# Gated linear attention and a low-rank mixer on one core: gates kept as logarithms on 64 partitions, decay matrices by one matmul and an Exp, scores and state products on four 64x64 tiles

## The chip, the cores and the metric

The kernel runs on one core of a Trainium2 chip. Its engines are TensorE (PE, with its weight loads as PEld), VectorE (DVE), ScalarE (ACT), GpSimd (POOL) and the queues that issue transfers (SP's and ACT's). The metric is the device time of one launch in microseconds (us).

## The reference

Two stages. First a recurrent attention over 768 steps for 4 batches and 8 heads of 40 channels; then a token mixer of rank 32 and an MLP 320 -> 1280 -> 320 over the 320 channels of each token. All in float32.

```python
for t in range(S):
    m_new = np.maximum(f_gate[:, :, t] + m, i_gate[:, :, t])
    f_stab = np.exp(f_gate[:, :, t] + m - m_new)
    i_stab = np.exp(i_gate[:, :, t] - m_new)
    m = m_new
    C = f_stab[:, :, None, None] * C + i_stab[:, :, None, None] * np.einsum('bhd,bhe->bhde', vt, kt)
    n = f_stab[:, :, None] * n + i_stab[:, :, None] * kt
    h_tilde = np.einsum('bhde,bhe->bhd', C, qt)
    denom = np.maximum(np.abs(np.einsum('bhd,bhd->bh', n, qt)[:, :, None]), 1.0)
    y[:, :, t] = o * h_tilde / denom          # o = sigmoid(o_gate)
...
u = x + (x.T @ U @ V).T                       # x: y with the heads side by side
out = u + np.maximum(u @ w_ch1, 0.0) @ w_ch2
```

## The kernel before

The recurrence is done in blocks of 64 steps: 768 steps are two halves (`hf`) of 384, a half is six blocks (`NQ`). Within a block the output is a masked product of scores (q times k), weighted with the decay between the two steps, times v (`pv`); what comes from earlier blocks goes through the state C (`inter`). The heads lie in two groups `m` of four, one on partitions 0 to 63, one on 64 to 127, so that one instruction on 128 partitions serves two heads; `i` counts the four pairs.

The work of a batch b and half hf, in the program's names:

- the gates, once for all batches, on 32 partitions for each half: scans for the running maximum, two exps, two more scans (`gate_max`, `gate_w`, `gate_g`), then products with the identity that turn the factors to token-major order (`tok`, `dect`).
- the decay matrix of a pair (128x384): a row of forget factors is spread over 64 partitions, for the first 12 pairs by a TensorE product with a one-column selector (`rowmm`, tensor `fst`), later by a broadcast transfer (`fd<-fsd`); then a scan on DVE (`decay_scan`, L753) runs along each row. The weight of the state (`gst`, `gsd`) is spread the same way and multiplied on q (`q_decay`, L748).
- `scores`: 12 products of 40 rows by 64x64 for a pair, on two of the four 64x64 tiles of TensorE; `weigh` (L772) multiplies them with the decay; `pv` and `inter` add into two PSUM banks on all four tiles; `kv` (k times v of a block, two tiles) and `state` (L694, L696) carry C from block to block.
- `norm`, `out_norm`, `gate` give x for a half (L825, L831). Then `rows` multiplies x with U (as two F32R parts), `cols` adds V's part and transposes x into `ut`, and the MLP follows as `up` (8 F32R products of 128x384 for each of 10 slices) and `down` (9 of 128x320). Weights come as float64 words and are turned into a high and a low F32R part by DVE and ACT (`cv`, L519, L521).

The order is not the code's order. `Plan` collects operations with a priority and an assumed cost, and `schedule` lists them engine by engine before the kernel is built; each engine then works its list strictly in order. Where TensorE would be idle by the planner's reckoning, it puts in products of zeros (`zeros`, fillers), which keep the engine active. PSUM has two pools, three banks for `down` and five for all else.

Of the kernel before, what the change touches and what calls it, by code (L numbers as in the profile page):

```python
# [19 lines left out]
RANK = 32  # L20
# [10 lines left out]
DMP = 3 * P  # L31


REBASE = 2.0 ** -112
SIGNED = -(2.0 ** 32)

# [8 lines left out]


FB_FROM, GB_FROM = 12, 8
LAG = 2
CV0, CV1, CV2 = 53.6, 80.0, 95.3
TICK, TICK_COLUMNS, FILL_NS, FILL_COLUMNS = 5120.0 / 3, 1900.0, 107.0, 256.0  # L50
RP, MP = 75.4, 175.5
GP = 21.3
ALT_PRI = 94.9
FILL_SLACK, FORCE, FILL_TO = 0.8, True, 2200.0

ORDER = {
    "gate": 20.0, "gate_w": 10.0, "part2": -70.0, "out_norm": -30.0, "part1": -10.0, "gate_turn": 10.0, "part3":
    -30.0, "rest1": 2.0, "w_low": 30.0, "vi": -10.0, "state": -4.0, "load_tk": -20.0, "w13_low":
    -30.0,
}  # L60
ORDER0 = {
    "rows": 25.0, "inter": 3.0, "x_low": -10.0, "weigh": 10.0,
}
BEGIN, COLD, FIRST_DMA, PE_SETUP = 600.0, 4500.0, 1700.0, 2200.0
DELTA = {"pe": 0}

WIDE_DMA = 630.0
# [7 lines left out]
    "prr": (1, [P, DM], F32R),  # L75
    "rru": (1, [P, HS], F32R),
    "kv": (2, [P, 2 * 3 * NP * (D + DV)], F32),
    "og": (2, [P, 2 * 3 * NP * D], F32),
    "v2": (1, [P, 2 * 3 * NP * DV], F32),
    "qd": (3, [Q + D, HS], F32),  # L80
    "qk": (3, [Q + D, 2, HS], F32),
    "C": (5, [Q + D, 3 * NP * DV], F32),
    "dm": (2, [P, HS], F32),
    "wt": (2, [P, HS], F32),
    "fd": (3, [P, HS], F32),
    "rd": (2, [P, 3 * NP], F32),
    "o": (3, [P, DM], F32),
# [4 lines left out]
BANKS = {"m2": 3, "ps": 5}  # L92
SHARE = {"dc": ("ps", 2), "st": ("ps", 5), "at": ("ps", 5), "m1": ("ps", 5)}
# [5 lines left out]
class Plan:  # L99


    def __init__(self, slots):
        self.slots = {tag: [[tile, 0.0, None, tag] for tile in tiles] for tag, tiles in slots.items()}
        self.ops, self.at, self.busy, self.port = [], {}, defaultdict(float), []
# [8 lines left out]
    def op(self, kind, pri, eng, cost, fn, r=(), w=(), new=(), stream="", load=1.0, port=False):  # L113
# [27 lines left out]
        self.port.append(port or not isinstance(eng, str))  # L141

    def keep_busy(self, at, start, cost, load, filler):

        busy = self.busy
        while True:
            n = int(at // TICK)
            step = FILL_NS * (2 if at < COLD else 1)
            if busy[n] >= FILL_TO:
# [3 lines left out]
            elif at + FILL_SLACK * step <= start:  # L153
                if filler(at):
                    busy[n] += FILL_COLUMNS
                at += step
            else:
                break
        while FORCE:
# [4 lines left out]
            if lack <= gain * max(0.0, left - cost) or left < FILL_NS or not filler(start):  # L164
                break
            busy[n] += FILL_COLUMNS
            start += FILL_COLUMNS / gain
        a, z = start, start + cost * (2 if start < COLD else 1)
        while a < z:
# [3 lines left out]
            a = b + 0.01  # L173
        return start

    def schedule(self, filler, ENGINE):

        ops = self.ops
        waits = [len(set(o[4]) | set(o[5])) for o in ops]
# [9 lines left out]
        while ready:  # L189
            picks = {}  # L190
            for n, est in ready.items():
# [3 lines left out]
                for key, tag in new:  # L195
# [4 lines left out]
                    s = max(s, open_at[nth]) if len(open_at) > nth and self.held[tag] + nth < most else float("inf")  # L200
# [4 lines left out]
                if isinstance(engs, str):  # L205
                    picks.setdefault(engs, []).append((max(s, free[engs]), pri, n))
# [15 lines left out]
            if eng == "pe":  # L222
                s = self.keep_busy(free["pe"], s, cost, load, filler)
# [43 lines left out]
def mlstm_mixer_kernel(  # L267
# [42 lines left out]
    ident6 = const.tile([P, HS], F32, name="ident6")  # L310
    ones = const.tile([NBH, Q], F32, name="ones")
    zeros = const.tile([P, 512], BF16, name="zeros")


    fst = const.tile([2 * NBH, HS + 1], F32, name="fst")
    gst = const.tile([2 * NBH, HS], F32, name="gst")
# [768 lines left out]
```

## Time and profile before

| | us |
|---|---|
| median of 3 runs | 389.26 (386.53, 389.26, 389.57) |
| profiled execution, span (no other time is listed for it) | 389.8 |
| TensorE busy in it | 379.4 (97%) |
| DVE busy | 219.1 (56%) |
| ACT busy | 106.9 (27%) |
| POOL busy | 61.1 (16%) |
| transfers | 40.65 MB, 104 GB/s in the mean |

A matmul's busy time is a modelled length of the pipeline, 0.31 to 0.34 us for one that is followed by the next after half of that; so the busy share of TensorE says little, and starts of neighbouring instructions are the measure. F32 products appear twice in the trace (768 records for 384 products), F32R products once.

### The profile page before, as it was taken

How to read it: one execution, taken by the hardware profiler on the slowest of the kernel's cores; microseconds unless marked ns; L12 is line 12 of the kernel's file. 1: busy time of each engine (PE TensorE's matmuls, PEld its weight loads, DVE VectorE, ACT ScalarE, POOL GpSimd, SP SyncE). 2: the span in 40 equal slices, each digit the busy share in tenths (PEclk: the TensorE clock that was granted, in tenths of full speed). 3: DMA queues.
4: the chain of work that ended last, by engine and by line, in shares of the span. 5: the costliest groups of instructions: out<-in, count | busy, mean ns of one | idle time of the engine just before them, and what ended most of it. 6: DMA issues, size and time to landing. Idle time of an engine off the chain costs nothing. (4 is left out here: it accounts for less than half of the span.)

```text
span 389.8 us, 11285 instructions
## 1 busy us (share of the span) xinstructions
PE 379.4 (97%) x4860; PEld 336.2 (86%) x4860; DVE 219.1 (56%) x471; ACT 106.9 (27%) x240; POOL 61.1 (16%) x65
## 2 busy tenths in 40 slices
PE   8999998899999899999999999999999999999996
PEld 5566666578898899999898899998999999999996
DVE  7747888745988853459886845256620433220322
ACT  4320235505453352102143113211420322220220
POOL 1303353521425200023231200000000000000000
PEclk9859999857999999999999999999999999999999
DMA  8963968836954921126978421020000010100001
GB/s 176 183 190 108 212 182 184 246 126 132 275 168 137 227 77 50 47 96 176 225 189 207 148 62 50 2 76 4 2 0 2 1 52 0 53 0 2 25 27 50
DMA packets 23002, 40.65 MB, mean 104 GB/s; under 512 B 4200, under 2 KB 15720, under 8 KB 22952
## 3 DMA queue, kind: packets, MB, share of 16 engines
q1 hardware_dynamic: 22760, 39.70, 38.3%
q8 instruction: 38, 0.62, 0.7%
q10 hardware_dynamic: 192, 0.23, 0.2%
q14 instruction: 12, 0.10, 0.1%
HBM read 35.68 MB, written 4.23 MB: 102 GB/s over the span
## 5 line engine op out<-in xcount | busy, mean ns | idle before, releaser
L290 PE MATMUL m<-w2h,h 128*128 128x320 f32 x480 | 120.4, 313 | 0.0
L290 PE MATMUL ps<-ut,w1h 128*128 128x384 f32 x400 | 118.2, 341 | 0.6 <-DVE ut L895 0.3
L934 DVE SCALAR_TENSOR_TENSOR h<-ps,h 128x384 fp32r<-128x384 f32 x80 | 44.0, 554 | 93.4 <-ACT h L932 92.6
L290 PEld LDWEIGHTS m<-w2h,h 128*128 128x128 f32 x480 | 83.5, 188 | 0.8
L290 PE MATMUL ps<-ut,w1l 128*128 128x384 f32 x240 | 80.6, 336 | 0.0
L932 ACT ACTIVATE h<-ps 128x384 fp32r<-128x384 f32 x80 | 38.9, 491 | 150.3 <-PE ps L290 98.7
L290 PEld LDWEIGHTS ps<-ut,w1h 128*128 128x128 f32 x400 | 73.6, 188 | 2.2 <-DVE h L934 0.7
L290 PE MATMUL m<-w2l,h 128*128 128x320 f32 x240 | 73.9, 308 | 0.0
L290 PEld LDWEIGHTS m<-w2l,h 128*128 128x128 f32 x240 | 45.1, 188 | 0.0
L290 PEld LDWEIGHTS ps<-ut,w1l 128*128 128x128 f32 x240 | 45.1, 188 | 0.0
L290 PEld LDWEIGHTS <-zeros 128*128 128x128 bf16 (+1 forms) x204 | 19.9, 111 | 17.6 <-issue 11.0
L290 PE MATMUL m<-zeros 128*128 128x256 bf16 x196 | 34.1, 315 | 0.0
L290 PE MATMUL ps<-qk 40*64 40x64 f32 x768 | 31.0, 227 | 0.3 <-DMA out<-o 0.3
L290 PEld LDWEIGHTS ps<-qk 40*64 40x64 f32 x768 | 27.1, 140 | 4.4 <-issue 2.2
L772 DVE TENSOR_TENSOR wt<-ps,dm 128x384 f32<-128x384 f32 x32 | 17.7, 552 | 15.1 <-PE ps L290 14.9
L753 DVE TENSOR_TENSOR_SCAN dm<-fd,ident 128x384 f32<-128x384 f32 x20 | 20.8, 1041 | 3.5 <-DMA fd<-fsd 3.4
L290 PEld LDWEIGHTS ps<-kv,wt 64*64 64x64 f32 x768 | 15.8, 143 | 6.6 <-issue 4.2
L957 DVE TENSOR_TENSOR o<-m,x 128x320 f32<-128x320 f32 x24 | 11.0, 487 | 18.3 <-PE m L290 18.2
L290 PEld LDWEIGHTS ps<-v,kv 64*40 64x40 f32 x704 | 15.7, 119 | 5.8 <-issue 5.0
L290 PE MATMUL ps<-v,kv 64*40 64x41 f32 x704 | 17.5, 204 | 2.9 <-issue 2.8
L659 POOL TENSOR_TENSOR v<-kv,tok 128x492 f32<-128x492 f32 x10 | 10.4, 1057 | 61.2 <-PE ps L290 57.2
L290 PE MATMUL ps<-kv,wt 64*64 64x41 f32 x768 | 19.7, 238 | 0.1
(91 smaller groups left out, 403.1 us busy)
## 6 DMA issues: line engine op xcount, KB each, us to landing
kv<-in_tk SPq DMA_DIRECT2D x16, 486.0 KB
qk<-in_qk SPq DMA_DIRECT2D x64, 120.0 KB
raw<-in_w SPq DMA_DIRECT2D x20, 320.0 KB
og<-in_tk SPq DMA_DIRECT2D x16, 240.0 KB
fd<-fsd SPq DMA_DIRECT2D x40, 96.0 KB
out<-o SPq DMA_DIRECT2D x24, 160.0 KB
fd<-gsd SPq DMA_DIRECT2D x24, 96.0 KB
fd<-gsd SPq DMA_DIRECT2D x24, 80.0 KB
```

The source lines that it names most:

```text
L290: nc.tensor.matmul(o, a, b, start=start, stop=stop, **kw)
L659: p.op("v2", at(n - 1), ("pool", "dve"), (pool(VO) * 0.79, dve(VO)), lambda e, e2=e2: e.tensor_mul(v2flat()[:, e2], vflat()[:, e2], tokv(1 ...
L753: lambda kfb=kfb, kdm=kdm: nc.vector.tensor_tensor_scan(T[kdm], T[kfb][:, 0:HS], ident6, 0.0, ALU.mult, ALU.add),
L772: p.op("weigh", at(u), "dve", dve(HS), lambda ks=ks, kw=kw, kdm=kdm: nc.vector.tensor_mul(T[kw], T[ks][:, 0:HS], T[kdm]), r=[ks, kdm], w=[ ...
L932: p.op("relu_high", pri + m - 1000, "act", 371, lambda: nc.scalar.activation(T[kh][:, 0, :], T[kp][:, 0:HS], AF.Relu), r=[kp], w=[(kh, 0)] ...
L934: p.op("relu_low", pri + m - 1000, "dve", dve(HS), lambda: nc.vector.scalar_tensor_tensor(T[kh][:, 1, :], T[kp][:, 0:HS], 0.0, f32(T[kh][: ...
L957: p.op("residual", pri - 1000, "dve", dve(DM), lambda: nc.vector.tensor_add(T[ko], T[ka][:, 0:DM], T[X][:, tt, 0:DM]), r=[ka] + [(X, hf, m ...
```

## The change

- Gates: both halves lie together on 64 partitions, and stay logarithms. `G` is the running sum of the log forget factors within a block, `E` the log input gate less G. Each is split into a high and a low F32R part, and stored to DRAM (`ggd`, `eed`); `gsd` holds exp(G).
- Decay matrix of a pair: one F32R product of 80 rows (`e`: a triangular mask with a large negative number, selectors, and the loaded rows of G and E) gives the logarithm of the decay with the input gate in it, 128x384 in PSUM, and ACT's Exp writes it to `dm`. The scan, the spread rows and the product of v with the input gate (`vi`) go. The state's weight is spread by a product and an Exp in batch 0 (`g_rows`), by transfers after that.
- `scores` does two pairs at once, 24 products on four tiles and into two banks; `kv` does all six blocks at once in the same manner, ACT copies the result (`kv_keep`), and `state` works on the copy, on DVE or POOL. The order of heads on the partitions alternates (`r ^ ip`).
- POOL builds the constant rows of `e` at the start (`put`). Sigmoid becomes Tanh and a POOL step. `norm` is on DVE alone. Batch 0's `rows` is one F32 product per chunk (`rows32`).
- One PSUM pool of eight banks; the planner knows a cost for going between whole-array and tiled products (`SWITCH`), and has a new table of priorities for all operations.

```diff
-BANKS = {"m2": 3, "ps": 5}
-SHARE = {"dc": ("ps", 2), "st": ("ps", 5), "at": ("ps", 5), "m1": ("ps", 5)}
+BANKS = {"ps": 8}
+SHARE = {"m2": ("ps", 3), "m1": ("ps", 3), "st": ("ps", 2), "at": ("ps", 4), "a0": ("ps", 8), "o": ("cv", 5)}
...
+            away = SWITCH * ((self.last != "F") + (mode != "F"))
...
+        p.op("gate_sum", -89, "dve", scan(HS), lambda: V.tensor_tensor_scan(G(), begin(), f(), 0.0, ALU.mult, ALU.add),
+             r=kf + [(X0, "one")], w=[(X0, "G")], port=True)
+        p.op("gate_e", -89, "dve", dve(HS), lambda: V.scalar_tensor_tensor(E(), i(), 64 * LEAST, G(), ALU.max, ALU.subtract),
+             r=ki + [(X0, "G")], w=[(X1, "E")], port=True)
...
+        p.op("store_g", -88, "sp", dma(NG * S * 4), lambda: nc.sync.dma_start(
+            out=ggd.rearrange("r l t -> r (l t)"), in_=part(X2, 0, S)), r=[(X2, "gh"), (X2, "gl")], w=[("ggd",)])
...
+            nc.gpsimd.affine_select(
+                t[0:Q, 0:4 * HS].rearrange("p (x s) -> p x s", s=Q), one.unsqueeze(2).to_broadcast([Q, 4 * NQ, Q]),
+                [[0, 4 * NQ], [-1, Q]], ALU.is_gt, 0.0, base=0, channel_multiplier=1)
...
-                p.op(
-                    "decay_scan", at(u), "dve", scan(HS),
-                    lambda kfb=kfb, kdm=kdm: nc.vector.tensor_tensor_scan(
-                        T[kdm], T[kfb][:, 0:HS], ident6, 0.0, ALU.mult, ALU.add),
...
+                        def load_er(m=m):
+                            nc.sync.dma_start(out=f32(T[ke][64 + 2 * m:66 + 2 * m, 0:4 * HS]).rearrange("p (h s) -> p h s", s=HS),
+                                              in_=ggd[r0 + 4 * m:r0 + 4 * m + 4].rearrange("h l t -> l h t"))
...
+                    p.op("decay", at(u), "pe", 173, lambda kd=kd, i=i: mm(T[kd][:, 0:HS], el(i), er(i)),
+                         r=[(ke, x, m) for x in "lr" for m in range(2)], w=[kd], new=[(kd, bank)], stream="att")
+                    p.op("decay_exp", at(u), "act", act(HS), lambda kd=kd, kdm=kdm: nc.scalar.activation(T[kdm], T[kd][:, 0:HS], AF.Exp),
+                         r=[kd], w=[kdm], new=[(kdm, "dm")])
...
                     for j in range(NQ):
                         cs = slice(j * Q, (j + 1) * Q)
+                        for ip in range(2):
+                            for r in range(2):
+                                m, rows = r ^ ip, slice(Q * r, Q * r + D)
+                                t = T[kqk][rows, ip]
+                                mm(T[ks[ip]][m * Q:(m + 1) * Q, cs], t[:, 1, cs], t[:, 0, cs], skip_group_check=True)
...
+                    for j in range(nk):
+                        for ih in range(0, NP, 2):
+                            for ip in range(2):
+                                for m in range(2):
+                                    r, o = slice(m * Q, (m + 1) * Q), (m ^ ip) * Q
+                                    mm(grid(T[kk[ip]], NQ, 2, DV)[o:o + D, j, ih // 2, :], ktv(r, j % 2, j // 2, ih + ip),
+                                       v2v(r, j % 2)[:, j // 2, ih + ip, :], skip_group_check=True)
...
+                            if n == 0:
+                                e.tensor_mul(T[kx], t[:, c], dect[0:Q + D, hb, :, j].unsqueeze(2).to_broadcast([Q + D, NP, DV]))
+                            else:
+                                e.tensor_add(T[kc][:, j], T[kc][:, j], T[kx])
...
+            if b == 0:
+                p.op("rows32", base + RP, "pe", 560, lambda c=c: mm(
+                    T[kp][:, 0:DM], uf(c), T[X][:, c, 0:DM], start=(c == 0), stop=(c == NC - 1)),
+                    r=[(X2, "uf")] + rx, w=[kp], new=[(kp, "st")] if c == 0 else [], stream="mix")
+                continue
```

TensorE's list at the place where the first `up` stands. Before, an `inter` block of batch 1 ends, the `cols` groups of batch 0 follow, and a `pv` block begins:

```order
L290 MATMUL ps_137<-C_106,qd_101 64x41
L290 MATMUL ps_136<-C_106,qd_101 64x41
L290 MATMUL ps_134<-vst,pst_91 128x384
L290 MATMUL ps_134<-cst,x_83 128x128 x3
L290 MATMUL ps_135<-vst,pst_91 128x384
L290 MATMUL ps_135<-cst,x_83 128x128 x3
L290 MATMUL ps_137<-kv_95,wt_114 64x41
```

After, the `kv` block of batch 1 ends, and `cols`, one decay product and the first `up` follow:

```order
L340 MATMUL ps_122<-v_0_94,kv_91 40x41 x2
L340 MATMUL ps_118<-vst,pst_88 128x384
L340 MATMUL ps_118<-cst,x_79 128x128 x3
L340 MATMUL ps_121<-e_102 128x384
L340 MATMUL ps_124<-vst,pst_88 128x384
L340 MATMUL ps_124<-cst,x_79 128x128 x3
L340 MATMUL ps_119<-vst,pst_88 128x384
L340 MATMUL ps_119<-cst,x_79 128x128 x3
L340 MATMUL ps_117<-ut_82,w1h 128x384
```

What moved: between the last `rows` product of batch 0 and its first `cols` stood three score blocks, a `kv`, two `pv` and three `inter` blocks and 23 fillers of batch 1's first half; now it is two `pv` blocks and one `kv` block.

DVE's list in the first half of batch 1 (before) and the second half of batch 0 (after); `dm` is the decay matrix, `wt` the weighted scores. Before:

```order
L772 TENSOR_TENSOR wt_113<-ps_138,dm_111 128x384
L521 SCALAR_TENSOR_TENSOR cv_126<-raw_125,cv_126 128x320
L748 TENSOR_TENSOR qd_100<-qk_103,fd_116 104x320
L856 TENSOR_TENSOR h_90<-x_83,h_90 128x320
L856 TENSOR_TENSOR h_87<-x_83,h_87 128x320
L753 SCALAR_TENSOR_TENSOR dm_112<-ps_138,ident_64 128x384
```

After:

```order
L815 TENSOR_TENSOR gq_95<-qk_97,gq_95 112x768
L915 TENSOR_TENSOR x_79<-ps_117,og_93 128x3x160
L820 TENSOR_TENSOR dm_104<-ps_122,dm_104 128x384
L915 TENSOR_TENSOR x_79<-ps_118,og_93 128x3x160
L820 TENSOR_TENSOR dm_105<-ps_120,dm_105 128x384
```

What moved: no scan (listed as SCALAR_TENSOR_TENSOR with `ident`) stands on DVE any more, and the weighting writes over the decay matrix.

SP's list in the gate stage, where the transfers that the first decay matrix needs are issued. Before, the stores of the factors:

```order
L718 DMA qk_105<-in_qk 40x768
L426 DMA fsd<-fst 32x384
L718 DMA qk_105<-in_qk 40x768
L653 DMA og_98<-in_tk 128x480
L445 DMA gsd<-gst 32x384
```

After, stores and the first loads of `e`:

```order
L484 DMA gsd<-x_80 64x384
L767 DMA kv_91<-in_tk 64x2x976
L474 DMA eed<-x_80 64x768
L472 DMA ggd<-x_81 64x768
L767 DMA kv_91<-in_tk 64x2x976
L615 DMA vsd<-cv_113 128x192
L767 DMA kv_92<-in_tk 64x2x976
L741 DMA e_102<-ggd 2x4x384
L745 DMA e_102<-eed 12x4x64
```

What moved: the first decay matrix was made from `fst` on chip and needed none of these; now it needs both stores and the loads behind them.

## Rows read from the trace of the kernel before

**Rows 1.** The page, part 1: busy us, share and instructions.

```profile
PE 379.4 (97%) x4860; PEld 336.2 (86%) x4860; DVE 219.1 (56%) x471; ACT 106.9 (27%) x240; POOL 61.1 (16%) x65
```

**Rows 2.** Busy time by stretch: each engine busy us (instructions), PEclk, DMA share, GB/s.

```profile
0.00:10.00 10.00, 8.80 (x61) 5.12 (x62) 7.71 (x19) 4.55 (x6) 1.60 (x8) 1.00 0.81 178
10.00:20.00 10.00, 10.00 (x120) 5.81 (x120) 7.43 (x13) 3.87 (x7) 3.48 (x4) 0.86 1.01 180
20.00:75.30 55.30, 52.35 (x1087) 35.64 (x1085) 40.91 (x94) 18.91 (x47) 18.58 (x19) 0.93 0.73 187
75.30:92.30 17.00, 17.00 (x218) 12.08 (x216) 8.32 (x16) 4.02 (x9) 5.00 (x6) 0.50 0.37 107
92.30:386.30 294.00, 291.01 (x3382) 277.57 (x3379) 153.99 (x331) 75.57 (x173) 32.44 (x30) 1.00 0.30 83
386.30:389.80 3.50, 0.25 (x2) 0.00 (x0) 0.78 (x2) 0.00 (x0) 0.00 (x0) 0.92 0.38 140
```

**Rows 3.** Timeline of 56 to 93 us: start us, us, instruction [idle before, releaser].

```profile
66.00 0.35 ACT L831 COPY x<-x 128x192 f32<-128x192 f32 x1 [1.05 <-DVE x L825]
...
71.14 0.61 DVE L849 TENSOR_TENSOR pst<-ps,prr 128x320 fp32r<-128x320 f32 x2
...
79.94 0.56 DVE L772 TENSOR_TENSOR wt<-ps,dm 128x384 f32<-128x384 f32 x1 [2.22 <-PE ps L290]
...
87.12 0.69 PE L290 MATMUL ps<-vst,pst 128*128 128x384 f32 x1
...
92.33 0.42 PE L290 MATMUL ps<-ut,w1h 128*128 128x384 f32 x1
```

**Rows 4.** The chain that ended last, 240 to 262 us: start us, us, what.

```profile
248.01 1.41 PE ps L290 x8
249.42 1.31 PE m L290 x9
```

**Rows 5.** Timeline of TensorE, 257 to 266.5 us.

```profile
257.44 0.91 PE L290 MATMUL ps<-qk 40*64 40x64 f32 x24
258.28 0.42 PE L290 MATMUL m<-w2h,h 128*128 128x320 f32 x1
...
259.80 1.08 PE L290 MATMUL ps<-v,kv 64*40 64x41 f32 x45
...
261.09 0.89 PE L290 MATMUL ps<-qk 40*64 40x64 f32 x24
261.82 0.78 PE L290 MATMUL ps<-v,kv 64*40 64x41 f32 x32
...
265.43 0.56 PE L290 MATMUL ps<-kv,wt 64*64 64x41 f32 x24
265.80 0.91 PE L290 MATMUL ps<-qk 40*64 40x64 f32 x24
```

**Rows 6.** Groups of DVE instructions by line and form: busy us, mean ns.

```profile
L753 DVE TENSOR_TENSOR_SCAN dm<-fd,ident 128x384 f32<-128x384 f32 x20 | 20.8, 1041 | 3.5 <-DMA fd<-fsd 3.4
L694 DVE TENSOR_TENSOR C<-C,dect 104x164 f32<-104x164 f32 x40 | 17.7, 443 | 3.6 <-ACT C L692 3.4
L772 DVE TENSOR_TENSOR wt<-ps,dm 128x384 f32<-128x384 f32 x32 | 17.7, 552 | 15.1 <-PE ps L290 14.9
L696 DVE TENSOR_TENSOR C<-C,ps 104x164 f32<-104x164 f32 x40 | 12.6, 314 | 2.9 <-PE ps L290 2.5
L521 DVE SCALAR_TENSOR_TENSOR cv<-raw,cv 128x320 uint32<-128x320 uint32 x20 | 11.1, 561 | 0.0
```

**Rows 7.** Timeline of the gate stage, 0 to 30 us.

```profile
0.74 0.41 POOL L377 MEMSET x<- 64x384 f32 x1 [0.29 <-POOLq L1075]
...
3.51 1.01 DVE L408 TENSOR_TENSOR_SCAN x<-x,x 32x384 f32<-32x384 f32 x1 [0.77 <-DMA x<-in_fig]
...
9.10 0.86 PE L290 MATMUL ps<-fst,cst 32*64 32x384 f32 x4
...
9.47 1.06 POOL L437 TENSOR_TENSOR x<-x,x 32x384 f32<-32x384 f32 x1 [7.81 <-DVE x L432]
```

More of the change, by code (lines that the diff above doesn't have):

```diff
@@ L31 @@
 DMP = 3 * P
+NG = 2 * B * NHEAD
+KW = NP * 3 * (D + DV)
+KP = KW + 4
+GW = KW + NP * 3 * D
+QR = 48
+EROW = 80
 REBASE = 2.0 ** -112
 SIGNED = -(2.0 ** 32)
+NEVER = 2.0 ** 100
+LEAST = -120.0
 C_IDENT = 0
@@ L141, in op, with keep_busy @@
         self.port.append(port or not isinstance(eng, str))
-    def keep_busy(self, at, start, cost, load, filler):
-        busy = self.busy
+        self.mode.append(mode)
+    def keep_busy(self, at, start, cost, load, mode, filler):
+        busy, turn = self.busy, 0.0
         while True:
@@ L222, in schedule @@
             if eng == "pe":
-                s = self.keep_busy(free["pe"], s, cost, load, filler)
+                s = self.keep_busy(free["pe"], s, cost, load, self.mode[n], filler)
             for key, tag in new:
@@ new lines, in half, with pvmm @@
+                for ip in range(2):
+                    i = 2 * pg + ip
+                    kw = ("dm", b, hf, i)
+                    def pvmm(kw=kw, i=i):
+                        for j in range(NQ):
+                            for m in range(2):
+                                r = slice(m * Q, (m + 1) * Q)
+                                mm(num(m, j, i), T[kw][r, j * Q:(j + 1) * Q], vv(r, j % 2)[:, j // 2, i, :],
+                                   start=(i == 0 and j < 2), skip_group_check=True)
+                    p.op("pv", at(u + 2), "pe", 372, pvmm, r=[kw, (kt, 0), (kt, 1)] + ([("first", b, hf)] if i else []),
+                         w=[(x, i) for x in kn] + ([("first", b, hf)] if i == 0 else []),
+                         new=[(x, bank) for x in kn] if i == 0 else [], stream="att", load=0.8, mode="T")
@@ new lines, in half @@
+                p.op("kv", at(n - 0.5), "pe", 15.2 * 16 * nk, kvmm, r=[(kt, 0), (kt, 1), (kv2, 0), (kv2, 1)],
+                     w=kk, new=[(x, bank) for x in kk], stream="att", load=0.8, mode="T")
+                for ip in range(2):
+                    p.op("kv_keep", at(n - 0.5), "act", act(nk * 2 * DV), lambda ip=ip, kk=kk: nc.scalar.copy(
+                        T[kc][:, 0:nk, ip::2], grid(T[kk[ip]], NQ, 2, DV)[0:Q + D, 0:nk]),
+                        r=[kk[ip]], w=[(kc, x, ip) for x in range(nk)], new=[(kc, "C")] if ip == 0 else [])
@@ L968, in mlstm_mixer_kernel @@
     nc.vector.memset(zeros, 0.0)
-    nc.vector.memset(ones, 1.0)
-    for t in tiles["qk"]:
-        nc.vector.memset(t[32:Q, 0, :], 0.0)
+    for tag in ("qk", "gq"):
+        for t in tiles[tag]:
+            nc.gpsimd.memset(t[32:Q, 0:2, 0] if tag == "qk" else t[32:Q], 0.0)
     for bank in tiles["ps"]:
-        mm(bank[0:Q, :], zeros[:, 0:Q], zeros)
+        for c in range(2):
+            mm(bank[:, c * 256:(c + 1) * 256], zeros[:, 0:P], zeros)
     nc.scalar.copy(w1l[64:P, 2, :], zeros[64:P, 0:1].to_broadcast([P - 64, DFF]))
```

654 lines of the change are left out of this document (342 added, 312 removed).

## The prediction, made before the changed kernel ran

> **What bounds the kernel now.** I read the page's engine line first, and distrust it: TensorE is 97% busy [rows 1], but a busy time is a pipeline's length, and fillers count too. So I cut the span by where the MLP begins. The timeline has the first `up` product at 92.33 us [rows 3]; the table of stretches then shows two regimes [rows 2]. From 92.3 to 386.3 us, 294.0 us, TensorE runs at full clock (2.4 GHz) without a gap worth naming: that part lasts as long as its list of products. Before 92.3 it does not: DVE is at 74% in 20 to 75.3 us (40.91 of 55.30), transfers at 0.73 to 1.01 of their engines, TensorE's list has 189 fillers (counted in the orders, as all counts below), and the clock is at the lower level (1.2 GHz) for 17 us. So the time is three terms: H, when the first `up` begins; the list from there; and 3.5 us from the last product to the last store [rows 2]: 92.3 + 294.0 + 3.5 = 389.8, the span, half a us above the median of the runs.
>
> In H, the timeline shows x of batch 0 complete at 66.0, U's part of the mixer (`pst`) at 71.14 + 0.61, but the first `cols` only at 87.12 [rows 3]: TensorE's list puts batch 1's attention between, and that waits for DVE's scans while DVE in turn sat idle up to 2.2 us for TensorE, at half clock.
>
> **The list behind the first `up`.** I cost each product by starts of neighbours, not by durations. Eight `up` take 1.41 us (0.176 each), nine `down` 1.31 (0.146) [rows 4]; 640 and 720 of them make 112.8 + 104.8 = 217.6 us, and the change touches none. `cols`, the 36 `rows` and V's products stay too. What differs is attention. A score block of 12 takes from 261.09 to 261.82, 0.73 us, 61 ns a product; a `pv` block of 12 from 265.43 to 265.80, 31 ns; a `kv` of 24 with a `pv` between 259.80 and 261.09, so 1.29 - 0.37 = 0.92 us, 38 ns [rows 5]. Going back to whole-array products costs 258.28 - 257.44 - 0.73 = 0.11 us [rows 5]; I take as much for each change of mode, either way.
>
> The rows tell what four tiles give. Scores stream 64 columns, `kv` 41, both on two tiles: 61 to 38 is 64 to 41, so two tiles are bound by columns. `pv` streams 41 on four tiles and takes 31, not half of 38, so something else holds it there. Scores on four tiles are therefore bounded by 31 (half of 61 is 30) and by 61; I take 31, and for `kv` also 31 between 31 and 38.
>
> Before, behind the first `up`: scores 240 x 61 = 14.6 us, `kv` 216 x 38 = 8.2, `pv` 240 x 31 = 7.4, `inter` 234 x 31 = 7.3, 80 changes of mode 8.8: 46.3. After: scores 264 x 31 = 8.2, `kv` 216 x 31 = 6.7, `pv` and `inter` 264 x 31 = 8.2 each, 21 decay products at an `up`'s 0.176 = 3.7, 54 changes 5.9: 40.9. So 5.4 us less, though two more pairs' work stands behind. The 294.0 us also hold some 10 us of waits. These I keep, and add 1 for a crowd on DVE: of its list, rows 101 to 183 (the conversion of 12 of 22 weight parts, batch 1's attention, the first `relu` steps) add up to 41 us by their groups' means, against 43 us of TensorE's list in the same piece of program (112 `up` 19.7, 90 `down` 13.2, 10 of attention and mixing). **Term: 294.0 - 5.4 + 1 = 289.5 us** (285.5 if the waits shrink by 4, 291.5 if they grow by 2).
>
> **H, in three steps.** First, the start of attention. Before, the first decay row is spread at 9.10 us [rows 7], straight from SBUF. Now G and E must go to DRAM and come back. On SP, 4.5 MB are ahead of the loads of `e` (qk 1.2, og 0.5, kv 1.5, gates, constants, u and v 0.7, the three stores 0.5, vsd 0.1), in queues that moved 178 to 180 GB/s when nearly full [rows 2]: 25 us. TensorE's own list holds 145 fillers ahead of the first decay product; before did 61 products, mostly fillers, in its first 10 us [rows 2], so 24 us for 145. DVE's gate chain from 3.51 us [rows 7] is no longer than that: two scans of 1.0, five steps of 0.55, a third scan, and so some 10 to 13. POOL's `put` is unseen in the trace: 4,400 elements per partition, between 0.41 us for 384 (a memset) and 1.06 (a product) [rows 7], so 5 to 12 us, beside the transfers. I take 26, bounds 19 (if the transfers run ahead of the stores) and 31 (fillers at half clock). The 17 us that this costs against 9.1 have no cover, but conversions of u, v and the first weights move into them.
>
> Second, DVE from the first weighting (26 + 2.5) to `pst`. The scans of about 1 us [rows 6] are gone, 13 of the 32 from the head, and the products of v with the input gate. DVE's list from there to `pst` is 31.9 us by the means of the groups view, of which rows 6 has the longest forms: 10 weightings 5.5, 15 steps of the state 5.6 (7 by 0.44, 8 by 0.31), 6 weight parts with 7 low parts 9.0, q's decay 2.5, normalizing and gating 6.1, v2 2.0, `vst` and `pst` 1.2. Before, DVE was 74% busy in the like stretch [rows 2]; at that share 31.9 us take 43. So `pst` stands at 71.6. ACT has some 33 us of work up to the same point, in a list that feeds DVE; I let DVE's share stand for both.
>
> Third, `cols` and `ut`: before 92.33 - 87.12 = 5.2 us [rows 3], at half clock and with a `pv` between. Now two `pv` blocks and a `kv` (2.2 us) run while DVE writes `pst`, then `cols` follows; I take 2.3. The 15 us between `pst` and `cols` of before are gone, because that work now stands behind the first `up`, counted above. **H = 74** (59 with DVE at 90% from 19 us, 88 at 62% from 31).
>
> A rule on the side: DVE's add to the state took 0.31 us with its input in PSUM, the multiply with both inputs in SBUF 0.44 [rows 6]. The GPSIMD Engine Reference of the Trainium skill, Specifications, says that a DVE instruction with two SBUF inputs contends with GpSimd for SBUF. Now both steps have SBUF inputs, and POOL does a part of them: by it those 8 adds take 0.44 each, 1 us more on DVE, and H is 75.4. No row shows the add in this form; I stay with 74.
>
> **Sum: 74 + 289.5 + 3.5 = 367 us**, 23 below the profiled execution.
>
> **Rivals.** *DVE closes up.* If scans and the spread rows were what made it wait, it runs at 90% from 19 to 26 us on and H is 59 to 66: 348 to 356 us with some waits in the list gone too. For it: the waits in 75 to 92 us are for score blocks behind slow spread rows. Against: the chain of states and the two `norm` steps stay serial.
>
> *The start is later.* With `put` at its upper bound and the loads of `e` behind bulk transfers the first decay product comes at 40, not 26: 381 us. For it: queues at 1.01 in 10 to 20 us [rows 2], and every wait on SP now holds back the loads behind it.
>
> *Four tiles don't overlap*, the change that isn't what it says. The two row tiles of a pair write one bank at different partitions. If that serializes, scores stay at 61 ns and `kv` at 38: 264 x 30 + 216 x 7 = 9.4 us in the list, some 2 of the 4.6 in the head (120 x 30 + 136 x 7): 378 us. Against: the two tiles of before share a bank too, and their time went by columns [rows 5]. The Trainium skill, TensorEngine Tiling (Array Packing), Restrictions and Gotchas, states that different row tiles cannot access the same PSUM bank at once; by that rule this rival would hold, and the trace of before speaks against it.
>
> *Slower: TensorE starves in the first MLP.* From the first `up` on the list has no filler (15 before). DVE's 41 us there at 74% last 55 against TensorE's 43; while it waits the clock can fall, as it did in 75.3 to 92.3 us at 0.50 [rows 2]. The 43 us of that piece at half clock cost 43 more: 410 us. It turns slower than before, by more than 1%, from 27 us of such a stretch. Against: after 92.3 us TensorE stayed at full clock [rows 2], with 154 us of DVE's work beside it.
>
> **How the numbers follow.** The forecast (357 to 377) has 0.58, DVE closing up 0.14, the later start 0.11, tiles that don't overlap 0.08, the starved MLP 0.06, and 0.03 is for a mixture that ends within 1% of before; 1% is about what a measurement of this kernel tells from no change. Faster by over 1%: 0.58 + 0.14 + 0.11 + 0.08 = 0.91; within 1% 0.03; slower 0.06. The range goes from 348 (H 59, and 285.5 behind it) to 383 (H 88 with 291.5).
>
> **What would show it.** The first `up` at 74 us and a start of `cols` within 3 us of `pst`; the first decay product near 26; score blocks of 24 in about 0.74 us (1.46 if tiles don't overlap); 289 us from the first `up` to the last product, at full clock. I am wrong if DVE's share before the first `up` is far from 74%, if TensorE waits or slows in the 45 us behind it, or if the first decay product comes well after 31 us.

## The result, and the profile after

The changed kernel takes 371.56 us in the median of four runs (369.09 to 374.81), the one before 389.41: a ratio of 0.956, with a 95% interval of 0.946 to 0.965. In a later comparison it was 372.30 against 389.21, 0.965 (0.958 to 0.973). Ratios, here and below, are taken over the faster executions of each kernel alone (those of the kernel before lie from 381 to 393 us), so they aren't the quotients of the medians beside them. 367 us had been forecast, with a range of 348 to 383. The forecast is a sum of spans; the profiled execution of the changed kernel took 369.90 us with a span of 368.2, so 367 stands against 368.2.

Part 1 of the page of the changed kernel, in the columns of [rows 1]:

```profile
PE 343.4 (93%) x4754; PEld 319.8 (87%) x4754; DVE 187.2 (51%) x425; ACT 123.0 (33%) x268; POOL 51.9 (14%) x81
```

Its stretches, in the columns of [rows 2], cut at the first decay product, at `pst`, at the first `up` and at the last product:

```profile
29.08:69.07 39.99, 33.61 (x927) 26.23 (x927) 27.87 (x70) 20.30 (x48) 10.06 (x12) 0.91 0.79 187
69.07:71.89 2.82, 2.82 (x128) 2.71 (x119) 1.93 (x6) 1.99 (x6) 0.00 (x0) 1.00 0.42 60
71.89:364.30 292.41, 284.30 (x3543) 272.81 (x3541) 144.87 (x326) 90.95 (x201) 27.71 (x40) 0.99 0.35 85
364.30:368.20 3.90, 0.34 (x3) 0.08 (x1) 0.87 (x2) 0.00 (x0) 0.00 (x0) 1.00 0.35 126
```

The three terms are H 71.9, list 292.4 and tail 3.9; before they were 92.3, 294.0 and 3.5. So H gives 20.4 us and the list behind it 1.6. How much of the 20.4 is work stays open. The 92.3 us of before hold 17 us at the lower clock [rows 2], and the mean granted clock of that execution was 0.964, which makes 28 us at the lower clock in all; 12 of 31 later executions of the same kernel took 380.9 to 386.2 us at means of 0.982 to 0.991, which make 7 to 14 us (estimates from the means). None of the 12 was profiled. By the ratios of 0.965 and 0.971 that were taken beside them, the gain is some 11 to 13 us and not 18.

The timeline of the same kernel shows where in H, against [rows 3]:

```profile
66.57 0.35 ACT L921 COPY x<-x 128x192 f32<-128x192 f32 x1 [4.39 <-DVE x L915]
...
69.07 0.62 DVE L939 TENSOR_TENSOR pst<-ps,rru 128x320 fp32r<-128x320 f32 x2 [1.38 <-ACT rru L956]
...
70.17 0.44 PE L340 MATMUL ps<-vst,pst 128*128 128x384 f32 x1
...
71.89 0.42 PE L340 MATMUL ps<-ut,w1h 128*128 128x384 f32 x1
```

x of batch 0 is complete at nearly the same time as before (66.6 for 66.0), though attention begins at 29.1 and not at 9.1. Then `cols` follows `pst` at once; before, 15.4 us of batch 1's attention stood between.

TensorE's blocks, at places where only one kind stands (against [rows 5]):

```profile
67.77 0.70 PE L340 MATMUL ps<-x,x 128*128 128x320 f32 x2
68.41 0.91 PE L340 MATMUL ps<-kv,dm 64*64 64x41 f32 x48
69.12 1.12 PE L340 MATMUL ps<-v,kv 64*40 64x41 f32 x96
70.17 0.44 PE L340 MATMUL ps<-vst,pst 128*128 128x384 f32 x1
...
99.13 0.93 PE L340 MATMUL ps<-qk 40*64 40x64 f32 x48
99.99 0.45 PE L340 MATMUL ps<-vst,pst 128*128 128x384 f32 x1
```

From start to start, less the 0.11 us of a change of mode, 24 score products take 0.75 us, 31 ns each (61 before), and 48 `kv` products 0.94, 20 ns each (38 before). The first row is one F32 product of the whole array over 320 columns, as two records (a record is an instruction as the trace lists it): 0.64 us less 0.11, so some 0.27 for a record.

So the list should have shrunk by more than 1.6 us. It did not, mostly because TensorE waits where it didn't before. The table of waits of TensorE behind the first `up` (us in total, times, longest), before:

```profile
PE ps L290 <- DVE h L856: 0.8, 1, 0.8
PE ps L290 <- DVE wt L772: 0.7, 1, 0.7
...
PE ps L290 <- issue: 0.2, 1, 0.2
```

and after:

```profile
PE ps L340 <- issue: 6.7, 3, 4.8
PE ps L340 <- DVE h L1028: 0.8, 1, 0.8
```

"issue" is a wait for nothing that the profile shows. The largest, in the timeline of the changed kernel:

```profile
121.27 0.89 PE L340 MATMUL ps<-C,gq 40*64 40x41 f32 x48
121.97 0.91 PE L340 MATMUL ps<-qk 40*64 40x64 f32 x48
127.71 1.52 PE L340 MATMUL ps<-C,gq 40*64 40x41 f32 x48 [4.83 <-issue]
129.16 0.63 PE L340 MATMUL ps<-w2h,h 128*128 128x320 f32 x1
```

The block is `inter`. The first of its weight loads ran at 122.64, so at least what its weights wait for was there; the next instruction came 5.0 us later, while DVE ended at 124.0 and ACT and POOL had nothing. The table of stretches around it:

```profile
110.00:122.67 12.67, 12.67 (x326) 11.59 (x325) 6.62 (x16) 5.12 (x11) 3.97 (x6) 1.00 0.78 181
122.67:127.71 5.04, 0.21 (x17) 0.10 (x7) 1.02 (x2) 0.00 (x0) 0.00 (x0) 0.92 0.42 87
127.71:134.00 6.29, 6.29 (x65) 6.21 (x65) 3.58 (x10) 1.02 (x3) 0.00 (x0) 0.52 0.34 91
```

After the wait the granted clock is 0.52, the lower level (1.2 GHz), for most of 6.3 us, which loses some 3 us more. The transfers of that wait, in the DMA view of 124.9 to 126.6 us (packets, MB, share):

```profile
q8 instruction: 1, 0.02, 5.0%
q1 hardware_dynamic: 8, 0.01, 3.0%
```

One transfer of 16 KB on a queue for instructions, from 125.13 to 126.48 us by the trace; TensorE goes on 1.2 us after it. The page counts 37 of these in the whole run, 0.61 MB, which is about 64 bytes for each of TensorE's 2 x 4754 records (products and weight loads). That gave a theory that the prediction had not held: TensorE runs ahead of its instructions. The kernel before has such a wait too, but in H, in the middle of a `kv` block:

```profile
74.25 0.58 PE L290 MATMUL ps<-v,kv 64*40 64x41 f32 x21 [1.56 <-issue]
```

### The profile page after: what moved, and what is told of

It is laid out like the page before. It is cut to its first block, busy times and chain, and to the rows that moved or that the text cites. A ratio compares the mean times of both kernels' runs of the same rounds, so it can differ in the third digit from the quotient of the medians.

```text
span 368.2 us, 10927 instructions
## 1 busy us (share of the span) xinstructions
PE 343.4 (93%) x4754; PEld 319.8 (87%) x4754; DVE 187.2 (51%) x425; ACT 123.0 (33%) x268; POOL 51.9 (14%) x81
## 4 chain that ended last, share of the span: by engine, by line
PE 82%; DMA 6%; DVE 6%; issue 3%; ACT 1%; POOL 0%; SPq 0%; DVEq 0%; POOLq 0%
PE ps L340 82%; DMA og<-in_tk 2%; DMA gq<-gsd 2%; DVE gq L815 2%; DMA raw<-in_w 1%; DMA x<-in_fig 1%; DVE dm L820 1%; ACT gq L801 0%; DVE x L915 0%; POOL x L454 0%; DVE w1l L665 0%; ACT dm L792 0%; DVE cv L586 0%; SPq L754 0%; DVE C L869 0%
## 5 line engine op out<-in xcount | busy, mean ns | idle before, releaser
L340 PE MATMUL ps<-w2h,h 128*128 128x320 f32 x480 | 123.0, 314 | 0.0
L340 PEld LDWEIGHTS ps<-w2h,h 128*128 128x128 f32 x480 | 84.6, 189 | 0.5
L340 PE MATMUL ps<-w2l,h 128*128 128x320 f32 x240 | 74.2, 309 | 0.0
L340 PEld LDWEIGHTS ps<-w2l,h 128*128 128x128 f32 x240 | 45.5, 190 | 0.0
L340 PE MATMUL ps<-zeros 128*128 128x256 bf16 x210 | 30.3, 306 | 2.3 <-DVE x L439 1.1
L340 PEld LDWEIGHTS <-zeros 128*128 128x128 bf16 x210 | 21.9, 109 | 8.0 <-issue 2.1
L1051 DVE TENSOR_TENSOR cv<-ps,x 128x320 f32<-128x320 f32 x24 | 11.1, 488 | 22.1 <-PE ps L340 22.1
L340 PE MATMUL ps<-C,gq 40*64 40x41 f32 x704 | 16.9, 238 | 5.2 <-issue 4.8
L340 PEld LDWEIGHTS ps<-kv,dm 64*64 64x64 f32 x768 | 15.4, 137 | 6.4 <-DVE dm L820 3.2
L340 PE MATMUL ps<-kv,dm 64*64 64x41 f32 x768 | 18.4, 232 | 2.5 <-DVE dm L820 1.8
L820 DVE TENSOR_TENSOR dm<-ps,dm 128x384 f32<-128x384 f32 x32 | 16.6, 548 | 6.4 <-PE ps L340 6.3
```

What stands on the lines that cost most here:

```text
L340: nc.tensor.matmul(o, a, b, start=start, stop=stop, **kw)
L820: p.op("weigh", at(u), "dve", dve(HS), lambda ip=ip, ks=ks, kdm=kdm: nc.vector.tensor_mul(T[kdm], T[ks[ip]][:, 0:HS], T[kdm]), r=[ks[ip]], ...
L1051: p.op("residual", pri - 1000, "dve", dve(DM), lambda: nc.vector.tensor_add(T[ko], T[ka][:, 0:DM], T[X][:, tt, 0:DM]), r=[ka] + [(X, hf, m ...
```

## The experiments

**The order alone.** The kernel before, with two numbers changed:

```diff
-RP, MP = 75.4, 175.5
+RP, MP = 75.4, 20.0
-        mlp(b, 0, base + 229.2)
+        mlp(b, 0, base + (229.2 if b else 110.0))
```

> The kernel before, with two priorities changed: cols of batch 0 and its first MLP half come ahead of what is left of batch 1's first attention half (list: 120 score, 108 pv and 88 inter products ahead of the first up, as in the changed kernel; before 144, 144 and 118). Scans, spread rows and two-tile products stay. Theory (most of the gain is the order): pst stays at 71, cols within 1 us behind it, first up at 74 to 77; the list behind it grows by the moved attention and 14 fillers to 297 to 302 us; 375 to 381 us in all, 8 to 14 below before. Rival (the order only pays once the scans are off DVE): TensorE waits more than 5 us for DVE in the 45 us behind the first up, and the clock falls there: 384 to 395 us.

390.6 us, ratio to before 1.022 (1.009 to 1.034): the order alone gains nothing. Its timeline and two stretches:

```profile
77.85 0.61 DVE L849 TENSOR_TENSOR pst<-ps,prr 128x320 fp32r<-128x320 f32 x2
...
82.24 0.44 PE L290 MATMUL ps<-ut,w1h 128*128 128x384 f32 x1
```

```profile
20.00:77.85 57.85, 55.33 (x1021) 36.93 (x1019) 37.99 (x86) 16.17 (x41) 16.30 (x16) 0.80 0.67 164
82.24:387.18 304.94, 300.49 (x3611) 285.39 (x3608) 162.70 (x345) 79.46 (x180) 36.27 (x34) 1.00 0.31 85
```

`cols` does follow `pst` by 1 us, and the first `up` comes 10 us earlier than in [rows 3]; but the list behind it is 11 us longer (304.9 for 294.0), at full clock. The work between `pst` and `cols` had to be done somewhere. `pst` itself came 6.7 us later with the same work on DVE (38.0 us): in the new list TensorE waits 2.3 us for a decay scan at 51 us, and its granted clock is 0.50 from 60 to 70. The rival's end of the forecast came true, by another way than it gave: the clock was not low behind the first `up`.

**Scores and `kv` on two tiles.** The changed kernel; in both blocks the loop over `ip` goes outermost, so that the two tiles of one pair alternate:

```diff
-                    for j in range(NQ):
-                        cs = slice(j * Q, (j + 1) * Q)
-                        for ip in range(2):
+                    for ip in range(2):
+                        for j in range(NQ):
+                            cs = slice(j * Q, (j + 1) * Q)
                             for r in range(2):
```

> The changed kernel, with the products of each score block and each kv block in another order, so that the two tiles of one pair come first, then the two of the other: same products, same lists around them. Theory (the price by tile): a score block of 24 takes 1.46 us instead of 0.75, a kv block of 48 products 1.8 instead of 0.92; 264 x 30 ns + 216 x 19 ns = 12 us more behind the first up, 2 to 4 more ahead of it: 384 to 387 us. Rival (four tiles run ahead of the supply of instructions, and give part of it back as waits): the waits of TensorE for nothing shown (5.0 us at 122.7, 1.6 at 208.4, and the half clock behind the first, 3.4) go, so only 4 to 8 us more: 375 to 380 us.

379.3 us, 0.987 of before (0.983 to 0.992): 8 us of the gain are gone. A score block takes 1.26 us (52 ns a product), 40 `kv` products 1.44 (36 ns). By these, 264 x 21 + 216 x 16 ns = 9.0 us would be lost behind the first `up`; that stretch grew by 6.1 (298.5), H by 4.3 against the first run of the changed kernel and by 1.6 against the second, below. The waits for nothing shown went from 8.3 to 6.3 us in all, the largest from 4.8 to 3.3. So both theories have their part: the tiles are worth what they take, and a part is given back to a supply that doesn't keep up.

**The scans back on DVE.**

```diff
+                    def weigh(ip=ip, ks=ks, kdm=kdm):
+                        nc.vector.tensor_tensor_scan(
+                            T[kdm], cst[:, 251:252].to_broadcast([P, HS]), T[kdm], 0.0, ALU.mult, ALU.add)
+                        nc.vector.tensor_mul(T[kdm], T[ks[ip]][:, 0:HS], T[kdm])
```

> The changed kernel, with a scan of 128x384 that leaves the decay matrix as it is put ahead of each of the 32 weightings on DVE (1.04 us each, as the decay scans before); the lists of all other engines stay. Theory (DVE sets the time up to pst): 10 of them stand ahead of pst, which comes 8 to 11 us later, first up at 80 to 83, the other 22 lie beside TensorE: 379 to 383 us. Rival (the gain is the order, the scans were covered): first up at most at 75, at most 375 us.

390.5 us, 1.022 of before (1.013 to 1.031): 19 us more than the changed kernel, and so more than the whole gain. The stretches from the first decay product to `pst`, and from the first `up` to the end:

```profile
28.23:78.46 50.23, 41.40 (x927) 31.70 (x927) 38.63 (x80) 20.26 (x48) 11.95 (x12) 0.73 0.64 153
81.29:384.37 303.08, 291.47 (x3544) 277.31 (x3542) 166.33 (x348) 90.92 (x201) 30.20 (x40) 0.97 0.33 82
```

and TensorE's waits in the second:

```profile
PE ps L340 <- DVE dm L823: 4.7, 8, 1.2
PE ps L340 <- DVE C L873: 2.3, 2, 1.4
```

The head did as expected: 10 more DVE instructions (80 for 70) with 10.8 us, and `pst` 9.4 later than in the first run of the changed kernel. Against its second run and its shifted form, both below, it is 6.7 and 7.5 us. The granted clock of this stretch fell too, to 0.73. Behind the first `up` both theories had the scans covered, and were wrong: 10.7 us (10.9 and 13.6 against the other two), at 55% of DVE's time. There a block of scores, a weighting and a `pv` follow each other, TensorE waits up to 1.2 us at a time for the weighted scores or the state, 7.0 us in these two rows, and the mean clock is 0.97 for 0.99.

**Both of these at once**, with the two edits above.

> The changed kernel with both earlier edits: an idle scan ahead of each weighting on DVE, and scores and kv on two tiles. What is left of the change is the later start, Exp for the decay, the new plan and the order. Theory (the prices add, 19 and 8 us on 371): 395 to 400 us, some 10 above before: the price of the later start and of the waits for instructions, which the two gains had to pay. Rival (the prices hide in each other, since TensorE waits for the scans with either tiling): 388 to 393 us.

391.4 us, 1.011 of before (1.000 to 1.022); the rival had it. With the scans on DVE the tiles are worth nothing (391.4 against 390.5); with them off, 8 us. The scans are worth 12 us on two tiles and 19 on four. These are differences of separate comparisons, and a us or two of them is noise. Neither half of the change has a price of its own.

**48 more products at the start of TensorE's list.**

```diff
+    for n in range(48):
+        mm(tiles["ps"][n % 8][:, 0:64], zeros[:, 0:P], zeros[:, 0:64])
```

> The changed kernel, with 48 more small products of zeros at the very start of TensorE's list, where it waits 5.6 us for the gates anyway: every later TensorE instruction stands 48 products (96 instructions) later in the instruction stream, nothing else changes. Theory (the 5.0 us wait at 122.7 us is for TensorE's next instructions, fetched in pieces of 16 KB): the wait no longer stands behind the first product of that inter block; it moves 48 records up, into the score block ahead of it, or shrinks, and the waits at 33, 38 and 208 us move likewise. Rival (the wait is for data of batch 1): it stays in the same inter block with 4 us or more. Time of the whole: 366 to 376 us by either.

371.2 us, 0.971 of before (0.963 to 0.980). The wait has left the `inter` block:

```profile
124.67 0.89 PE L340 MATMUL ps<-C,gq 40*64 40x41 f32 x48
127.17 1.12 PE L340 MATMUL ps<-qk 40*64 40x64 f32 x33 [1.61 <-issue]
```

It stands at the score block ahead, 48 records up in the program, and so at the same place of the stream (the window ends within that block, hence 33). The table of stretches from 0 to the last record ahead of a wait shows that place in the count of PE; the changed kernel:

```profile
0.00:33.39 33.39, 26.38 (x349) 21.29 (x350) 13.46 (x27) 12.43 (x22) 15.15 (x30) 0.85 0.78 175
...
0.00:122.67 122.67, 109.59 (x2005) 94.39 (x2006) 80.90 (x194) 59.05 (x131) 36.08 (x58) 0.93 0.78 183
0.00:208.38 208.38, 189.02 (x3153) 169.60 (x3154) 121.97 (x285) 82.77 (x182) 44.15 (x70) 0.94 0.64 149
```

and this one:

```profile
0.00:125.34 125.34, 114.25 (x2005) 98.29 (x2005) 81.12 (x192) 58.98 (x131) 35.82 (x58) 0.89 0.75 178
0.00:164.20 164.20, 151.50 (x2643) 134.18 (x2644) 101.91 (x241) 70.17 (x155) 40.84 (x65) 0.90 0.70 165
0.00:169.66 169.66, 155.84 (x2771) 138.14 (x2772) 105.56 (x250) 71.31 (x159) 40.84 (x65) 0.90 0.71 167
```

2643 is 2005 and five times 127.6, 2771 one piece of 128 records further, 3153 nine pieces from 2005. In between lie whole numbers of pieces of about 128 records with their weight loads, which are 16 KB: the waits stand where such a piece ends. Data of batch 1 as the cause is ruled out: the same `inter` block now runs through.

**The changed kernel again.**

> The changed kernel again, beside the other three of this call. If the waits for TensorE's instructions depend on the moment at which a fetch gets its turn, they stand at the same records (349, 2005, 3153) with other lengths than 1.9, 5.0 and 1.6 us, and the median stays at 369 to 374 us. If they were something else, they stand elsewhere or not at all.

372.3 us. The waits stand behind records 349, 2005 and 3153 as before, with 3.4, 5.1 and 2.2 us from start to start: the places are the program's, the lengths vary from run to run.

**Fewer bytes.** The loads of k, v and the ones column are cut for batches 1 to 3:

```diff
+                            nf = 8 if b else KP
-                            nc.sync.dma_start(out=T[kt][m * Q:(m + 1) * Q],
+                            nc.sync.dma_start(out=T[kt][m * Q:(m + 1) * Q, :, 0:nf],
```

> The changed kernel, which leaves out nearly all of the loads of k, v and the ones column in token order for batches 1 to 3 (8 of 976 elements a row are loaded; 12 transfers of 488 KB less, and what is computed there is from old data). All lists stay. Theory (the instruction fetch of 16 KB queues behind data): the fetch for the wait at TensorE's record 2005 starts 1 to 2 us after the one before it was used up, not 4.3, and the wait there falls from 5.0 to under 2 us; the clock stays up behind it: 363 to 368 us. Rival (the fetch is slow by itself, or the wait is for something else): the wait at record 2005 stays at 3 us or more: 370 to 373 us.

367.4 us, 0.951 of before (0.941 to 0.960). The fetch behind record 2005 started 1.8 us after the piece before was begun (4.3 and 4.0 in the two runs of the changed kernel), as a queue behind data would have it. It isn't shown by this alone: with all loads in place the same fetch started 2.7 us after that point in the shifted kernel and 1.7 in the one with the scans back. The wait was still 2.3 us from start to start, not under 2, and that at record 3153 2.3. Crossing, fetch, and 1.4 us from its landing to the next product made 4.2 us; 128 records of dense attention lasted 1.9 us (120.80 to 122.66 in the changed kernel). So TensorE outruns the supply even with these loads gone; what a queue adds is open.

**A rule against it.** The planner counts records and starts no more than 128 in a given time:

```diff
+PAGE, FETCH = 128, 3200.0
...
+    def supply(self, n, s):
+        most = PAGE - self.records(n)
+        z = s + self.ops[n][2]
+        had = 0
+        for t, k in reversed(self.issued):
+            if t <= z - FETCH:
+                break
+            had += k
+            if had > most:
+                return t + FETCH - self.ops[n][2] + 0.01
+        return s
```

> The changed kernel, with one more rule for TensorE in the planner: no more than 128 records (256 instructions, 16 KB) may start in any 3.2 us, so that dense attention blocks are separated by MLP products. The list is planned anew (222 fillers for 210, 66 changes of mode behind the first up for 54: 1.3 us more). Theory (TensorE outruns its instruction fetch): the waits for nothing shown behind the first up fall from 6.4 us to under 3, and the half-clock stretch behind the wait at 122.7 (3.4 us lost) goes: 364 to 369 us. Rival (the waits are for data, or the fetch isn't paced by products): they stay at 5 us or more, and the extra changes of mode are lost: 371 to 375 us.

370.5 us, 0.950 of before (0.938 to 0.962), not told apart from the changed kernel. One wait over 1 us was left behind the first `up`, 3.7 us at record 2643, where the fetch started 5.6 us after the crossing. The list took 289.8 us, 2.6 less; H 77.6, some 3 to 6 more. Its four times lie from 364.1 to 373.7 us and the profiled one took 372.9, so these two are rough. 3.2 us were too short.

Then with a longer time:

```diff
-PAGE, FETCH = 128, 3200.0
+PAGE, FETCH = 128, 5600.0
```

> The rule of 128 records again, now in any 5.6 us, since a piece of instructions took 3.3 us and more from the crossing into the one before to the landing, and 1.2 to 1.5 us more until TensorE went on. The list is planned anew: 88 changes of mode behind the first up for 54, one kv block moved behind it, 30 more fillers ahead. Theory (supply): no wait for nothing shown over 1 us behind the first up; at full clock there; 365 to 369 us. Rival (the rule costs more in changes of mode, 3.7 us, and in its order than the waits did): 370 to 376 us.

372.9 us, 0.965 of before (0.958 to 0.971). Here the theory is borne out behind the first `up`, in the stretches of this kernel and in all that TensorE waits for there:

```profile
0.00:81.42 81.42, 66.51 (x1146) 51.40 (x1147) 48.40 (x112) 35.59 (x76) 26.69 (x42) 0.81 0.74 178
81.42:367.49 286.07, 285.68 (x3640) 272.02 (x3638) 145.30 (x329) 88.80 (x193) 15.57 (x23) 1.00 0.33 80
```

```profile
PE ps L359 <- DVE ut L1008: 0.3, 1, 0.3
```

No wait for instructions, full clock, and a list of 286.1 us, 6 less, though it holds a `kv` block and 34 changes of mode more. But the rule also spread the attention of the head, where nothing but fillers stood to go between: the first `up` came at 81.4. The sum is no better. The rule behind the first `up` alone, with the head left as it was, would by these rows give a span of 72 to 75 + 286 + 3.9 = 362 to 365 us, an estimate; that was not tried.

**The start of attention.** First earlier, with POOL's gate constants ahead of `put`:

```diff
-    "put": -95.9,
+    "put": -5.0,
```

> The changed kernel, with one priority changed: POOL sets the constants of the gate stage before it builds the rows of e, not behind (2 more fillers, DVE's list as it is). DVE's scan for G then doesn't wait 3.8 us for POOL, the stores of E and G come some 3.5 us earlier. Theory (H hangs on the start of attention): first decay product at 25 to 26 instead of 29.1, pst and the first up 3 us earlier (about 69): 367 to 369 us. Rival (the loads of e stay behind the store of v's parts and the fillers, or the weights' conversion sets H): first decay at 28 or later or the first up at 71 or later: 370 to 373 us.

375.3 us, 0.972 of before (0.963 to 0.980). The first decay product came at 27.3 (29.1 and 27.9 in the two runs of the changed kernel), now waiting 1.3 us for a load of `e`; TensorE then lost 4.0 us at record 349 (1.9 in the changed kernel's first run, 3.4 in its second), and `pst` stood at 69.8. The rival's bounds for H (72.6 for the first `up`) held. The list was 296.6 us, 4.2 longer, with waits for instructions of 12.3 us in the whole run (8.3 and 11.1 in the two of the changed kernel).

Then with the rule of 3.2 us as well:

> Both edits together: the rule of 128 records in 3.2 us, and the constants ahead of the rows of e. If both theories hold, they add (waits of instructions behind the first up under 3 us, first up at 69): 361 to 366 us. If only one holds, 366 to 370; if neither, 371 to 375.

371.4 us, 0.964 of before (0.956 to 0.972): first decay product at 26.9, first `up` at 75.7, 290.9 behind it. Neither edit shows in the sum.

Then later, by 32 products of zeros ahead of the first decay product:

```diff
+                        if (b, hf, i) == (0, 0, 0):
+                            for n in range(32):
+                                mm(T[kd][:, 0:256], zeros[:, 0:P], zeros)
                         mm(T[kd][:, 0:HS], el(i), er(i))
```

> The changed kernel with 32 more products of zeros right ahead of the first decay product (0.107 us each at full clock, 0.148 as those before them: 3.4 to 4.7 us), so that attention starts later. Theory (no cover, as the prediction put it): pst and the first up come 3 to 5 us later, 374 to 377 us. Rival (conversions of weights and loads set H, DVE uses the time for them): the first up moves less than 2 us, 370 to 373 us.

370.3 us, 0.960 of before (0.951 to 0.968). The first decay product came at 31.3, the first `up` at 77.4: 3.4 and 2.9 us later than in the run of the changed kernel beside it. That fits an H that hangs on the start, but one pair doesn't show it: of the two runs of the changed kernel the one with the later start (29.1 for 27.9) had the earlier first `up` (71.9 for 74.6). The list took 287.7 us, 4.5 less; the pieces end at other products there, and no wait was over 2.1 us. So the whole was no slower, and a single run of 370 can't be read for an effect of 3 us unless its waits are counted.

## Why the prediction held, step by step

**H, first step, the start.** 26 was forecast with bounds of 19 and 31; it was 29.1. POOL's `put` took 8.3 us, within 5 to 12, and held the scan for G up by 3.8, which the prediction had put beside transfers. TensorE then waited 5.6 us for the gate stage, which the 24 us for its 145 fillers had not held, and the last 66 fillers ran from 19.6 up to the first decay product, partly at the lower clock (0.50 from 14.2 to 24.5 us). The loads of `e` were issued only at 22.1 us, since SP stood until 21.0 at the store of v's parts; no wait for them is shown, so TensorE's list came last and not the transfers.

**Second step, DVE to `pst`.** From the first weighting 43 us were forecast, 31.9 at a share of 74%. It started at 31.5, and `pst` came 37.6 us later, with 27.1 us of DVE's work, 72%. In the second run of the changed kernel it was 41.5 us with 27.2, 66%. Its stretch from the first decay product on, beside the like row above:

```profile
27.90:71.74 43.84, 37.56 (x927) 29.19 (x927) 27.97 (x70) 20.22 (x48) 10.12 (x12) 0.81 0.76 174
```

DVE's work is the same, 28.0 for 27.9, the stretch is 3.8 us longer, and the granted clock is 0.81 for 0.91. So the share isn't a constant that can be carried over from before: something else has a hand in this stretch, TensorE at the lower clock by these two rows, though no run tried that alone. The work was forecast 4 us too high and the share up to 8 points too high; that these and the later start cancel, 69.1 and 71.7 for 71.6, is luck. That DVE is one of the limits is shown by the idle scans: 10.8 us of them made `pst` 6.7 to 9.4 us later.

**Third step, `cols` and `ut`.** 2.8 us from `pst` to the first `up`, 71.9 in all where 74 was forecast; in the other runs of this kernel and of its shifted form 74.6 and 75.3. Right.

**The claim on the order** was half right. That the 15 us between `pst` and `cols` go, since that work stands behind the first `up`, is what the rows show, and the order alone is worth nothing, as that wording implies. But the sum then put the whole gain into DVE's work in the head. The runs show it in two halves: the scans cost 6.7 to 9.4 us in the head and 10.7 to 13.6 behind the first `up`, where the prediction had seen no price for them because TensorE waited only 0.7 us for weighted scores before. With the new lists that cover is gone.

**The list.** 289.5 was forecast, 292.4 measured. By starts of neighbours, attention fell from 43.9 to 39.8 us (the sum had 46.3 to 40.9), `kv` by more than the sum had (20 ns a product, not 31); fillers, V's and U's products and the transposes by 4; the MLP's own products took 1 more. The term that failed is "some 10 us of waits I keep, and add 1": what the steps between neighbours have over 0.6 us went from 0.9 to 6.3 us behind the first `up`, 5.4 of it at records 2005 and 3153, by the supply of instructions and not by a crowd on DVE, and the clock fell behind the largest. Nor were there 10 us of waits before: by the same starts the MLP's products took 225 us, not 217.6, and that is most of them. Errors of opposite sign make the 2.9.

**The side rule.** DVE's add to the state has both inputs in SBUF now; the groups view of the changed kernel by form:

```profile
L869 DVE TENSOR_TENSOR C<-C,cm 104x164 f32<-104x164 f32 x30 | 9.7, 323 | 0.6
...
L867 DVE TENSOR_TENSOR cm<-C,dect 104x164 f32<-104x164 f32 x25 | 9.1, 362 | 0.9 <-POOL C L869 0.4
```

The add takes 0.32 us (0.31 from PSUM, [rows 6]), not 0.44, so the 1 us that the prediction worked out did not come. But 0.44 was no price of two SBUF inputs. It is a mean of two cases. Of the 40 multiplies of before, 29 ran with no POOL instruction beside them and took 0.32 us each; eight lay beside one for most of their time and took 0.46 to 1.34, 0.93 in the mean. One of these, DVE's row and POOL's, each from its own timeline:

```profile
30.98 2.10 POOL L659 TENSOR_TENSOR v<-kv,tok 128x492 f32<-128x492 f32 x2 [13.47 <-PE ps L290]
32.12 1.13 DVE L694 TENSOR_TENSOR C<-C,dect 104x164 f32<-104x164 f32 x1
```

The changed kernel has one such multiply among its 25:

```profile
253.24 1.15 POOL L783 TENSOR_SCALAR og<-og 128x480 f32<-128x480 f32 x2
253.31 1.26 DVE L867 TENSOR_TENSOR cm<-C,dect 104x164 f32<-104x164 f32 x1 [0.18 <-POOL C L869]
```

None of its 30 adds lay beside a POOL instruction, so they don't test it. The adds of before with an input in PSUM took 0.29 to 0.33 us in the 12 cases that did. The GPSIMD Engine Reference, Specifications, of the Trainium skill states that DVE instructions with two SBUF inputs contend with GpSimd; the traces agree where the two overlap for most of the multiply's time. In the kernel before, the eight cost 4.9 us of DVE's time over 0.32 each, which the prediction did not see.

**The rivals.** DVE didn't close up: 64 to 70% from the first decay product to `pst`. The start was later, by 2 to 3 us and not by 14. The tiles overlap: 31 ns a product on four, 52 on two. That the two row tiles that write one bank overlap needs one number more, for both of these would also come out if only different banks ran side by side. A record over 320 columns takes 0.27 us, so one over 64 would take some 54 ns (an estimate); on two tiles, by the starts in the trace of that run, the records of the two row tiles come 7 ns apart and the next two 52 ns later, so two run in about the time of one. By the rule of TensorEngine Tiling (Array Packing), Restrictions and Gotchas, of the Trainium skill two row tiles could not use one bank at once; the trace disagrees. TensorE did starve, 6.7 us, for instructions and at 122 and 208 us rather than in the first MLP.

The Trainium skill, Runtime: NRT & Kernel Launch, Instruction fetch mechanics, states that instructions come in blocks of 16 KiB while the current one runs, and that the crossing costs little, mostly hidden. The 37 transfers of 16 KB agree with the first; the second holds for the MLP, and not for dense attention: waits of 1.6 to 5.1 us, start to start, at a crossing in the two runs of the changed kernel.

## What to carry to other kernels

Small products on four tiles are also small in time per instruction: count how long 256 instructions last, and put longer products between blocks where that is too short; here 1.9 us was, a rule of 3.2 left one wait and one of 5.6 none, though it cost as much elsewhere as it gave. A wait for "issue" in the middle of a block, at the same count of records in every variant, points to the supply of instructions; shift the stream by a few dozen products to prove it. And price the parts of a change together: taken out one at a time, scans and tiles were worth 19 and 8 us, and 19 together, because each was worth only what the other let through. And before a mean duration goes into a sum, look at its least and largest: a mean of 0.44 us was 0.32 with POOL idle and up to 1.34 with POOL at work.

## What was not expected of the hardware

`kv` products (weights of 64 rows and 40 columns) took 20 ns on four tiles, `inter` products (40 rows, 64 columns) 29, 0.70 us for 24 in the timeline of the wait; both stream 41 columns. What sets the difference was not tried. From the landing of a piece of instructions to the next product 1.2 to 1.6 us passed in the five waits at records 2005 and 3153 of the two runs of the changed kernel and of the shifted one.
